# Two-stage kernel on one core: product two of the second channel product added in PSUM to a ScalarE copy of product one, one addition over two banks, gates directly behind their additions

## The chip, the cores and the metric

The kernel runs on one core of a Trainium2 chip. The metric is device time in microseconds of one execution. Each core has TensorE (PE, matmuls; "PEld" are its weight loads), VectorE (DVE), ScalarE (ACT), GpSimd (POOL) and SyncE (SP, which here only issues DMAs). Matmul results land in PSUM: eight banks of 128 partitions by 512 float32. SBUF is the other on-chip memory. Every engine works through its own queue in order, and engines wait for each other on semaphores.

## The reference

For each of 8 batches (S = 3008 rows, D = 256), with no softmax:

```python
scores = np.matmul(z, z.transpose(0, 2, 1)) / S        # d_qk = 64
x = u * np.matmul(np.maximum(scores, 0.0) ** 2, v)     # gated attention
h = np.maximum(x.transpose(0, 2, 1) @ w_tok1, 0.0) @ w_tok2    # token mixer, 256 wide
u = x + h.transpose(0, 2, 1)
out = u + np.maximum(u @ w_ch1, 0.0) @ w_ch2           # channel mixer, 1536 wide
```

Inputs and output are float32; the kernel multiplies in bfloat16 and accumulates in float32.

## The kernel before

**Blocks.** Queries are cut into six blocks `q` of 512 columns (the last has 448), so `b, q` names a block of a batch. Attention of a block: TensorE makes transposed scores `sc` (L470), ScalarE takes the relu into `at` (L508 or L496), VectorE squares it in place (L516 or L547), TensorE multiplies it with `v` into `acc` (L697). The matmuls of `sc` and `acc` use half of the array's rows and run in pairs, one on each half. Thus `acc` ends as two banks, which have to be added: ScalarE copies one bank to SBUF (`cp`, L825), VectorE adds the other to it (L831) and multiplies with u, the gate (L851, and L856 for the last 64 columns), into `xT`. That is `finish` and `gate`. The copies `cp` live in three buffers (`res`), which they share with `u_sb`, the turned-back u of the mixer.

**Mixer.** Per batch: the first token product `a_ps` (L1058) with a chain of small steps on ScalarE and VectorE into `a_f`; the second, `h_ps` (L1128), whose result VectorE adds to `xT` (L1137); the first channel product `hp` (L1192), in six steps of four matmuls a block, each with a relu into `h2pre` (L1231, ScalarE); sums and differences of the quarters of `h2pre` in `hsum` (`make_sums`, L1383, L1388, L1401, VectorE); and the second channel product.

**Second channel product.** It is done by a scheme that needs seven block products in place of eight, numbered 1 to 7 (`product`, L1447). Products 1, 2 and 3 take `h2pre` as it is, the others its sums `hsum`. In full blocks a product is 12 matmuls of 128 columns; in block q = 5 it is 6. Results stand in four quarters `ro` (upper or lower rows `m`, left or right columns `h`). Product 1 goes to a bank of the tile `xb`; products 6, 7 and 4 go on accumulating in that bank. Products 2 and 5 with 3 use the two banks of the tile `zb`. Behind each product, `collect` has VectorE add its bank to a quarter of `ro` (L1480), the first time together with `u_sb`. So 6 waits for the addition of 1, 7 for that of 6, 4 for that of 7 and 3 for that of 5. All this is done for 47 blocks; the very last (batch 7, q = 5) is multiplied out plainly (`op`, L1544), as are the last rows of other blocks with q = 5.

**The order of the work.** The program is written out by a planner in Python. It keeps a clock for each engine (`free`), lists of operations that wait for an engine (`push`: when ready, how long, `first` for rank, `room` for buffers) and lists of TensorE pieces (`heads` for the token part, `tails` for the channel part) with what each needs. It issues whatever can start first by its own durations. The real engines then follow that order with semaphores. Within `tails` the order is fixed by hand: a tuple per kind of block, in which a number is a product, 0 is the next step of the first channel product of block q + 1 (`add_next`, "a zero" below), and a to d are four stages of a grouped first step (`grouped_ch1`, tile `gp`, L1312) that needs ScalarE copies (L1320, L1323), relus (L1327, L1331) and one custom addition of VectorE (L1338). PSUM tiles of two banks come from a ring of four slots.

The plain order holds for 19 blocks (b = 0: q = 0 to 4; other batches: q = 3 and 4), the grouped one for 21 (b > 0, q = 0 to 2), and `ORDER_LAST` for seven with q = 5, where pieces of the next batch's `a_ps` may run between products. One zero of a block is left over and runs in front of the next block's order.

## Time and profile before

| | |
|---|---|
| three runs | 1110.31, 1108.81, 1110.19 us; median 1110.19 |
| the profiled execution | 1109.13 us, span of its instructions 1107.3 us |
| TensorE clock granted | 1.000 |
| busy: TensorE, VectorE, ScalarE | 1102.2, 811.5, 684.7 us |
| matmuls | 11199 |
| `ro` additions (L1480) | 329: 56.3 + 37.4 + 18.9 + 18.7 = 131.3 us |
| HBM read and written | 65.4 and 24.6 MB |

A row of the timeline reads: start in us from the span's start, length, engine, line, operation, output <- inputs, shape, xcount, and in brackets how long the engine was idle before and what ended that. A group's row reads: line, engine, operation, names, shapes, xcount, then busy us and mean ns of one, then the idle time before the group's instructions and what ended most of it. The length of a matmul row reaches past its last matmul's streaming time, so the distance between starts says more than the length. A row of the view by windows has the window, its length, and for PE, PEld, DVE, ACT and POOL the busy us and count, then clock and DMA.

### The profile page before, as it was taken

The numbers are of one execution on the slowest core, as the hardware profiler recorded it, in microseconds if no ns is written. First come the engines' busy times: TensorE is split into PE (matmuls) and PEld (weight loads), VectorE is DVE, ScalarE is ACT, GpSimd is POOL, SyncE is SP. The second block draws the span as 40 slices with busy tenths as digits, with TensorE's granted clock in tenths as the row PEclk, the third lists the DMA queues.
The fourth block names the chain that finished last, engine by engine and source line by source line (L and its number), as shares of the span: only waits on it lengthen the run. The fifth ranks groups of instructions, "written<-read, shape, count | busy, mean of one in ns | idle before, by whom it ended". The sixth has DMA issues, their size and how long they took to land.

```text
span 1107.3 us, 27459 instructions
## 1 busy us (share of the span) xinstructions
PE 1102.2 (100%) x11199; PEld 695.2 (63%) x11199; DVE 811.5 (73%) x1791; ACT 684.7 (62%) x906; POOL 168.2 (15%) x386
## 2 busy tenths in 40 slices
...
PEclk9999999999999999999999999999999999999999
...
GB/s 179 167 199 184 149 96 152 127 179 146 190 127 149 190 133 177 127 156 191 140 189 120 133 218 141 170 122 150 198 160 169 116 145 185 125 160 104 64 59 96
DMA packets 465726, 165.55 MB, mean 150 GB/s; under 512 B 433024, under 2 KB 448960, under 8 KB 465600
## 3 DMA queue, kind: packets, MB, share of 16 engines
...
q10 hardware_dynamic: 512, 0.38, 0.1%
...
## 4 chain that ended last, share of the span: by engine, by line
PE 99%; DVE 0%; ACT 0%; issue 0%
PE acc L697 42%; PE hp L1192 19%; PE xb L1447 11%; PE zb L1447 8%; PE sc L470 6%; PE h_ps L1128 4%; PE a_ps L1058 3%; PE gp L1312 3%; PE op L1544 2%; PE first_acc L614 1%; PE wp L210 0%; DVE at L516 0%; ACT at L508 0%; DVE zr L183 0%; PE first_acc L189 0%; DVE zT L1850 0%
## 5 line engine op out<-in xcount | busy, mean ns | idle before, releaser
L697 PEld LDWEIGHTS <-v_sb 64*128 64x128 bf16 x4418 | 245.7, 94 | 212.5 <-issue 1.3
L1231 ACT ACTIVATE h2pre<-hp 128x1024 bf16<-128x1024 f32 (+1 forms) x245 | 239.9, 1005 | 182.7 <-PE hp L1192 180.5
L697 PE MATMUL acc<-at,v_sb 64*128 64x512 bf16 (+1 forms) x2738 | 341.6, 374 | 0.0
L508 ACT ACTIVATE at<-sc 128x1024 bf16<-128x1024 f32 (+1 forms) x290 | 286.8, 1027 | 72.0 <-PE sc L470 66.4
L516 DVE TENSOR_TENSOR at<-at 128x1024 bf16<-128x1024 bf16 (+1 forms) x290 | 198.1, 687 | 112.1 <-ACT at L508 107.9
L1192 PE MATMUL hp<-xT,w_ch_sb 128*128 128x512 bf16 (+1 forms) x984 | 238.3, 374 | 0.0
L697 PE MATMUL acc<-fl,v_sb 64*128 64x512 bf16 (+1 forms) x1680 | 193.0, 367 | 0.0
L1192 PEld LDWEIGHTS <-w_ch_sb 128*128 128x128 bf16 x984 | 90.8, 98 | 79.0 <-issue 2.6
L1447 PEld LDWEIGHTS <-hsum 128*128 128x128 bf16 x2088 | 127.9, 98 | 19.6 <-issue 0.5
L470 PE MATMUL sc<-zT 64*128 64x512 bf16 (+1 forms) x732 | 132.4, 359 | 0.1
L1383 DVE TENSOR_TENSOR hsum<-h2pre 128x1024 bf16<-128x1024 bf16 (+1 forms) x141 | 90.0, 647 | 22.7 <-ACT h2pre L1231 12.6
L825 ACT COPY cp<-acc 128x512 f32<-128x512 f32 (+1 forms) x94 | 54.9, 584 | 79.9 <-PE acc L697 69.0
L831 DVE TENSOR_TENSOR cp<-acc,cp 128x512 f32<-128x512 f32 (+1 forms) x94 | 63.4, 675 | 54.8 <-ACT cp L825 54.0
L1447 PEld LDWEIGHTS <-h2pre 128*128 128x128 bf16 x1566 | 93.8, 98 | 10.0
L496 ACT ACTIVATE at<-sc 128x512 bf16<-128x512 f32 (+3 forms) x152 | 56.2, 450 | 29.2 <-PE sc L470 28.8
L1447 PE MATMUL xb<-shared_sb,hsum 128*128 128x128 bf16 x1044 | 73.6, 219 | 0.0
L1480 DVE TENSOR_TENSOR ro<-xb,u_sb 128x256 f32<-128x256 f32 (+1 forms) x141 | 56.3, 400 | 17.9 <-PE xb L1447 17.7
L470 PEld LDWEIGHTS <-zT 64*128 64x128 bf16 x732 | 42.4, 94 | 41.6 <-issue 3.8
L129 POOL CAST mark<-at 128x1 f32<-128x1 bf16 x24 | 9.3, 386 | 388.1 <-DVE at L516 388.1
L851 DVE TENSOR_TENSOR xT<-cp,uT 128x512 bf16<-128x512 f32 (+1 forms) x94 | 62.4, 663 | 0.8
L547 DVE TENSOR_TENSOR at<-at 128x512 bf16<-128x512 bf16 (+3 forms) x152 | 41.0, 320 | 23.8 <-ACT at L496 23.8
L1401 DVE TENSOR_TENSOR hsum<-h2pre,hsum 128x512 bf16<-128x512 bf16 (+1 forms) x141 | 55.1, 400 | 4.1 <-ACT h2pre L1331 2.5
...
## 6 DMA issues: line engine op xcount, KB each, us to landing
...
```

What stands on the lines that cost most here:

```text
L470: nc.tensor.matmul(sc[:, r, c0:c1], zT[h, k:k + P], zT[h, m + c0:m + c1], start=True, stop=True)
L496: nc.scalar.activation(a3[:, i, c0:c1], sc[:, r, c0:c1], ACT.Relu, scale=inv_S)
L508: nc.scalar.activation(view, sv, ACT.Relu, scale=inv_S)
L516: nc.vector.tensor_mul(view, view, view)
L697: nc.tensor.matmul(o, vs[blk.b, g][rows, i, dh * P:(dh + 1) * P], rhs, start=(dh, h) not in blk.begun, stop=stop, skip_group_check=True)
L831: nc.vector.tensor_add(cp[:, :W], acc[:, 0, :W], cp[:, :W])
L851: nc.vector.tensor_mul(xT[:, dh, :full * P].rearrange("p (t s) -> p t s", s=P), acc[:, :full * P].rearrange("p (t s) -> p t s", s=P), uT[: ...
L1192: nc.tensor.matmul(hps[r % len(hps)][:, r, :W], w_ch1_sb[:, dc, cc * P:(cc + 1) * P], xT[:, dc, :W], start=(dc == 0), stop=(dc == DT - 1))
L1231: nc.scalar.activation(h2[:, :, :W], hp[:, :, :W], ACT.Relu)
L1383: nc.vector.tensor_sub(sums["s"][:, 0:2, :, :n * P], h[:, :, 1], h[:, 0])
L1447: nc.tensor.matmul(to[:, i * P:(i + 1) * P], lhs, weights[:, c2, :], start=(first_use and c2 == 0 and i == 0), stop=(c2 == CHT // 2 - 1), ...
L1480: nc.vector.tensor_add(res(m, h), source, us(m, h) if opening else res(m, h))
```

## The change

Product 2 now goes to the second bank of `xb`. Behind product 1, ScalarE copies the first bank to the second (`fork`), and product 2 accumulates on that copy: the second bank then holds product 1 + product 2, while 6, 7 and 4 go on accumulating in the first. `zb` is opened at product 5 and uses one bank. The additions of 1 and 2 are gone; behind product 4 one addition takes both banks of `xb` and u into both upper quarters. Products 2 and 6 need the copy; product 2 also has to let reads of `xb` finish that are already issued (`Read`), and reads still waiting on VectorE are set behind it. The orders are new, and the planner's figure for the relu is 0.95 in place of 0.92. In the attention part the gate is ranked 0.12 us earlier, and a copy `cp` is issued only while copies and `u_sb` tiles together hold under three buffers.

In words, the plain order was (0, 0, 1, 2, 0, 6, 5, 0, 7, 3, 0, 4) and is (0, 1, 0, 5, 2, 6, 0, 0, 7, 0, 3, 4).

```diff
@@ -33,6 +33,17 @@
     @property
     def t(self):
         return None if self.done.t is None else self.done.t - self.us
+
+
+class Read:
+
+
+    def __init__(self, done):
+        self.done = done
+
+    @property
+    def t(self):
+        return self.done.t or 0.0
 
 
 class Op:
@@ -820,6 +831,7 @@
         on_act = blk.b > 0 or load("act") + 0.46 < load("dve") + 0.67
 
         def copy(t):
+            copies[0] += 1
             cp = sb.tile([P, QW], F32, tag="res", name="cp", bufs=3)
             if on_act:
                 nc.scalar.copy(cp[:, :W], acc[:, 1, :W])
@@ -829,16 +841,18 @@
 
         def add(cp, t):
             nc.vector.tensor_add(cp[:, :W], acc[:, 0, :W], cp[:, :W])
-            push("dve", t, 0.58, 0.7, lambda t: gate(blk, dh, cp, t), first=1,
+            push("dve", t - 0.12, 0.58, 0.7, lambda t: gate(blk, dh, cp, t), first=1,
                  room=(lambda: (blk.b, blk.q) in uTs and has_room(("xT",))) if dh == 0
                  else lambda: (blk.b, blk.q) in xTs)
 
         engine, busy = ("act", 0.46) if on_act else ("dve", 0.66)
-        push(engine, end + 0.21, busy, busy + 0.15, copy, first=1)
-
-    gated = [0]
+        push(engine, end + 0.21, busy, busy + 0.15, copy, first=1,
+             room=lambda: copies[0] + live["us"] < 3)
+
+    gated, copies = [0], [0]
 
     def gate(blk, dh, acc, t):
+        copies[0] -= not blk.whole
         b, q, W = blk.b, blk.q, blk.W
         uT = uTs[b, q]
         if dh == 0:
@@ -1021,9 +1035,11 @@
 
     hid_done = Done()
     BORROW = 3
-    GROUPED = ("a", 0, 1, 2, "b", 6, 5, 0, "c", 7, 3, 0, 4, "d")
+    RELU = 0.95
+    GROUPED = ('a', 0, 1, 0, 'b', 2, 6, 5, 'c', 7, 3, 0, 'd', 4)
+    PLAIN = (0, 1, 0, 5, 2, 6, 0, 0, 7, 0, 3, 4)
     VERY_LAST = (B - 1, NQ - 1, CHT // 2 - 1)
-    ORDER_LAST = ((1, 2, 6, 5, 7, 0, 3, 4), (1, 2, 6, 5, 0, 7, 3, 0, 4))
+    ORDER_LAST = ((1, 2, 6, 5, 7, 0, 3, 4), (1, 6, 0, 5, 2, 0, 3, 7, 4))
 
     def add_mixer(b):
         st = {}
@@ -1238,7 +1254,7 @@
                         late_sums.append(lambda t: make_sums(q, c2 // 2, t))
                     else:
                         make_sums(q, c2 // 2, t)
-            engine, busy = ("act", 0.92) if on_act else ("dve", 1.15)
+            engine, busy = ("act", RELU) if on_act else ("dve", 1.15)
             ring.append((push(engine, end + 0.21, busy, busy + 0.16, evacuate,
                               done=h2_done[q, c2]), slots[0]))
             if c2 == CHT // 2 - 1:
@@ -1414,9 +1430,9 @@
 
         def bank_of(q, k):
 
-            if k in (2, 5, 3):
-                return st["zb", q][:, int(k != 2)]
-            return st["xb", q][:, 0]
+            if k in (5, 3):
+                return st["zb", q][:, 0]
+            return st["xb", q][:, int(k != 2)]
 
         def product(q, k, end):
 
@@ -1425,7 +1441,7 @@
             if k == 1:
                 st["x_slot", q], _ = take_slot()
                 st["xb", q] = bank_pair(st["x_slot", q], "xb")
-            if k == 2:
+            if k == 5:
                 st["z_slot", q], _ = take_slot()
                 st["zb", q] = bank_pair(st["z_slot", q], "zb")
             to = bank_of(q, k)
@@ -1435,7 +1451,7 @@
             weights = {1: w2[:, :, 0, 0, :], 2: w2[:, :, 1, 0, :], 4: w2[:, :, 1, 1, :],
                        3: w_mix_sb[:, 3], 5: w_mix_sb[:, 0], 6: w_mix_sb[:, 1],
                        7: w_mix_sb[:, 2]}[k]
-            first_use = k in (1, 2, 5)
+            first_use = k in (1, 5)
             for c2 in range(CHT // 2):
                 d, j = divmod(c2, 2)
                 for i in range(n):
@@ -1452,6 +1468,11 @@
                 done_with_h2(q)
                 for d in range(CHT // 4):
                     release(home_of(q), [1], end + 0.2)
+            if k in (2, 6, 7, 4):
+                behind = [taken[q, j] for j in (1, 6, 7)]
+                for op in waiting["dve"]:
+                    if op.done in behind:
+                        op.ready = max(op.ready, end + 0.21)
             collect(q, k, end)
 
         def collect(q, k, end):
@@ -1467,19 +1488,33 @@
             def us(m, h):
                 return st["u", q][:, h, m * n:m * n + n, :]
 
-            blocks_of = {1: (0, 0), 2: (0, 0), 5: (1, 1), 6: (1, 0), 3: (1, 0), 7: (1, 1),
-                         4: (0, 1)}
-            opening = k in (1, 5, 6, 4)
+            blocks_of = {5: (1, 1), 6: (1, 0), 3: (1, 0), 7: (1, 1)}
+            begins = k in (6, 5, 4) and ("asked", q) not in st
+            if begins:
+                st["asked", q] = True
+
+            def fork(t):
+                nc.scalar.copy(bank_of(q, 2)[:, :n * P], bank_of(q, 1)[:, :n * P])
+
+            def first_column():
+                m, h = blocks_of.get(k, (0, 0))
+                return st["res", q][:, m * n, h * P:h * P + 1]
 
             def add(t):
-                if k == 1:
+                if begins:
                     home, n_home = take_home(q)
                     st["res", q] = sb.tile([P, QW // P, D], F32, tag=home, name="ro",
                                            bufs=n_home)
-                m, h = blocks_of[k]
-                nc.vector.tensor_add(
-                    res(m, h), source, us(m, h) if opening else res(m, h))
-                recent[0] = st["res", q][:, 0, :1]
+                if k == 4:
+                    nc.vector.tensor_add(
+                        st["res", q][:, :n, :].rearrange("p i (h d) -> p h i d", d=P),
+                        st["xb", q][:, :, :n * P].rearrange("p h (i d) -> p h i d", d=P),
+                        st["u", q][:, :, :n, :])
+                else:
+                    m, h = blocks_of[k]
+                    nc.vector.tensor_add(
+                        res(m, h), source, us(m, h) if k in (5, 6) else res(m, h))
+                recent[0] = first_column()
                 over[q] -= 1
                 if not over[q]:
                     nc.sync.dma_start(
@@ -1491,18 +1526,23 @@
             ready = end + 0.21
             done = taken[q, k]
             if k == 1:
+                push("act", ready, busy, busy + 0.15, fork, first=2, done=done)
+            elif k == 2:
+                pass
+            elif begins:
                 with_u(q, ready, lambda at: push(
                     "dve", at, busy, busy + 0.15, add, first=1, room=(home_of(q),),
                     frees=frees_of(q), done=done))
             else:
-                done = push("dve", ready, busy, busy + 0.15, add, first=1, done=taken[q, k],
-                            room=lambda: ("res", q) in st)
+                us_ = busy if k != 4 else 0.62 if n == 2 else 0.34
+                push("dve", ready, us_, us_ + 0.15, add, first=1, done=done,
+                     room=lambda: ("res", q) in st)
             if k == 3:
                 ring.append((done, st["z_slot", q]))
             if k == 4:
                 ring.append((done, st["x_slot", q]))
 
-        over = [7] * NQ
+        over = [5] * NQ
         us_uses = [[1] for _ in range(NQ)]
         s_done = {(q, d, k): Done() for q in range(NQ) for d in range(CHT // 4) for k in range(4)}
         taken = {(q, k): Done() for q in range(NQ) for k in range(1, 8)}
@@ -1641,8 +1681,10 @@
         def add_product(q, k):
             needs = {
                 1: [Sooner(h2_done[q, c], 0.111 * c) for c in range(CHT // 2)] + w_done[2:],
-                2: [], 5: [mix_done, taken[q, 2]], 6: [taken[q, 1]], 3: [taken[q, 5]], 7: [taken[q, 6]],
+                2: [taken[q, 1]], 5: [mix_done], 6: [taken[q, 1]], 3: [taken[q, 5]], 7: [taken[q, 6]],
                 4: [taken[q, 7]]}[k]
+            if k == 2:
+                needs = needs + [Read(taken[q, j]) for j in (6, 7)]
             kind = {5: 0, 7: 1, 6: 2, 4: 3}.get(k)
             if kind is not None:
                 needs = needs + [Sooner(s_done[q, d, kind], 0.222 * d) for d in range(CHT // 4)]
@@ -1650,7 +1692,7 @@
                 needs = needs + [tok1_over[b + 1]]
             cost = pairs_of(q) * (CHT // 2) * column_time(P)
             tails.append(Piece(cost, needs, lambda end: product(q, k, end), opens=k == 1,
-                               closes=k == 4, key=(b, 2 + q), slot=k in (1, 2),
+                               closes=k == 4, key=(b, 2 + q), slot=k in (1, 5),
                                joins=k == 1 and q == NQ - 1))
 
         added = [0] * (NQ + 1)
@@ -1670,7 +1712,7 @@
                 us_uses[q][0] += bool(rest)
                 h2_uses[q] += bool(rest)
                 for k in (ORDER_LAST[b % 2] if q == NQ - 1 else GROUPED if grouped(q + 1) else
-                          (0, 0, 1, 2, 0, 6, 5, 0, 7, 3, 0, 4)):
+                          PLAIN):
                     if isinstance(k, str):
                         add_grouped(q + 1, 0, "abcd".index(k), q)
                     elif k:
```

The lines below are in the order in which the engines' queues hold them. ScalarE in the first grouped cycle of batch 1, before; L1323 and L1320 belong to stage a, L1327 and the next L1320 to b, L1331 to d, L1231 are relus of `hp`:

```order
L1323 COPY s_3507<-gp 128x512
L1320 COPY gp<-gp 128x512
L1231 ACTIVATE h2pre<-hp 128x1024
L1327 ACTIVATE h2pre<-gp 128x512
L1320 COPY gp<-gp 128x512
L1231 ACTIVATE h2pre<-hp 128x1024 x2
L1331 ACTIVATE h2pre<-gp 128x512
L1231 ACTIVATE h2pre<-hp 128x1024
```

The same place after:

```order
L1339 COPY s_3506<-gp 128x512
L1336 COPY gp<-gp 128x512
L1497 COPY xb<-xb 128x256
L1247 ACTIVATE h2pre<-hp 128x1024
L1343 ACTIVATE h2pre<-gp 128x512
L1336 COPY gp<-gp 128x512
L1247 ACTIVATE h2pre<-hp 128x1024 x2
L1347 ACTIVATE h2pre<-gp 128x512
```

The copy of `xb` stands behind the copies of stage a and ahead of the relu of the zero in front of product 1.

VectorE in the second grouped cycle of batch 2, before (`ro<-xb,u_sb` are the additions of 1, then 6; `ro<-zb,ro` of 2, then 3; `ro<-zb,u_sb` of 5; `ro<-xb,ro` of 7; the `ISA` row is the custom addition behind stage c; `t_sums` prepare the next group):

```order
L1383 TENSOR_TENSOR hsum<-h2pre 128x1024
L1388 TENSOR_TENSOR hsum<-h2pre,hsum 128x512
L1480 TENSOR_TENSOR ro<-xb,u_sb 128x2x128
L1401 TENSOR_TENSOR hsum<-h2pre,hsum 128x512
L1480 TENSOR_TENSOR ro<-zb,ro 128x2x128
L1480 TENSOR_TENSOR ro<-xb,u_sb 128x2x128
L1480 TENSOR_TENSOR ro<-zb,u_sb 128x2x128
L1268 TENSOR_TENSOR t_sums<-xT 128x512
L1273 TENSOR_TENSOR t_sums<-xT,t_sums 128x256
L1338 ISA h2pre<-gp,s_5761 128x2x512
L1480 TENSOR_TENSOR ro<-xb,ro 128x2x128
L1480 TENSOR_TENSOR ro<-zb,ro 128x2x128
```

and after (L1515 are the additions of 6, 5, 7 and 3, L1509 the one over two banks):

```order
L1404 TENSOR_TENSOR hsum<-h2pre,hsum 128x512
L1417 TENSOR_TENSOR hsum<-h2pre,hsum 128x512
L1284 TENSOR_TENSOR t_sums<-xT 128x512
L1289 TENSOR_TENSOR t_sums<-xT,t_sums 128x256
L1294 TENSOR_TENSOR t_sums<-xT,t_sums 128x256
L1515 TENSOR_TENSOR ro<-xb,u_sb 128x2x128
L1515 TENSOR_TENSOR ro<-zb,u_sb 128x2x128
L1354 ISA h2pre<-gp,s_5704 128x2x512
L1515 TENSOR_TENSOR ro<-xb,ro 128x2x128
L1515 TENSOR_TENSOR ro<-zb,ro 128x2x128
L1399 TENSOR_TENSOR hsum<-h2pre 128x1024 x2
L1509 TENSOR_TENSOR ro<-xb,u_sb 128x2x2x128
```

The sums are no longer parted by additions of 1 and 2, and the `t_sums` stand ahead of the additions of 6 and 5.

VectorE in an attention stage, before:

```order
L831 TENSOR_TENSOR cp<-acc_6320,cp 128x512
L516 TENSOR_TENSOR at<-at 128x4x256
L851 TENSOR_TENSOR xT<-cp,uT 128x512
L831 TENSOR_TENSOR cp<-acc_6338,cp 128x512
L547 TENSOR_TENSOR at<-at 128x512
L547 TENSOR_TENSOR at<-at 128x384
L851 TENSOR_TENSOR xT<-cp,uT 128x512
```

and after:

```order
L843 TENSOR_TENSOR cp<-acc_6307,cp 128x512
L865 TENSOR_TENSOR xT<-cp,uT 128x512
L527 TENSOR_TENSOR at<-at 128x4x256
L843 TENSOR_TENSOR cp<-acc_6323,cp 128x512
L865 TENSOR_TENSOR xT<-cp,uT 128x512
L558 TENSOR_TENSOR at<-at 128x512
L558 TENSOR_TENSOR at<-at 128x384
```

Squares that stood between an addition and its gate now stand behind the gate.

## The prediction

> **What bounds the kernel now.** I read the page first, then TensorE's rows in order of time in the stages that the change touches, then VectorE's and ScalarE's rows in the same stages, and last the groups by form, for durations. The page:
>
> ```profile
> span 1107.3 us, 27459 instructions
> PE 1102.2 (100%) x11199; PEld 695.2 (63%) x11199; DVE 811.5 (73%) x1791; ACT 684.7 (62%) x906; POOL 168.2 (15%) x386
> PEclk9999999999999999999999999999999999999999
> PE 99%; DVE 0%; ACT 0%; issue 0%
> ```
>
> PE is busy throughout at a full granted clock, and the chain that ended last is PE. A busy PE could still hide short waits, because matmuls overlap. So I read starts, not busy times. This is one whole cycle of a mixer stage that runs in the order without groups, from one product 1 to the next:
>
> ```profile
> 880.12 0.83 PE L1447 MATMUL xb<-w_ch_sb,h2pre 128*128 128x128 bf16 x12
> 880.79 0.83 PE L1447 MATMUL zb<-w_ch_sb,h2pre 128*128 128x128 bf16 x12
> 881.46 1.03 PE L1192 MATMUL hp<-xT,w_ch_sb 128*128 128x512 bf16 x4
> 882.32 0.83 PE L1447 MATMUL xb<-shared_sb,hsum 128*128 128x128 bf16 x12
> 882.99 0.83 PE L1447 MATMUL zb<-shared_sb,hsum 128*128 128x128 bf16 x12
> 883.66 1.03 PE L1192 MATMUL hp<-xT,w_ch_sb 128*128 128x512 bf16 x4
> 884.53 0.83 PE L1447 MATMUL xb<-shared_sb,hsum 128*128 128x128 bf16 x12
> 885.20 0.83 PE L1447 MATMUL zb<-shared_sb,h2pre 128*128 128x128 bf16 x12
> 885.87 1.03 PE L1192 MATMUL hp<-xT,w_ch_sb 128*128 128x512 bf16 x4
> 886.73 0.83 PE L1447 MATMUL xb<-w_ch_sb,hsum 128*128 128x128 bf16 x12
> 887.40 2.54 PE L1192 MATMUL hp<-xT,w_ch_sb 128*128 128x512 bf16 x12
> 889.78 0.83 PE L1447 MATMUL xb<-w_ch_sb,h2pre 128*128 128x128 bf16 x12
> ```
>
> Each product takes 0.67 us from its start to the next start (56 ns a matmul), and each four hp matmuls 0.86 us (215 ns each). No row starts later than the one before allows: the cycle is streaming and nothing else. The changed kernel has the same 11199 matmuls, so time can be won only where PE waits. Read in this way, the mixer stages have 17 spots at which a matmul starts more than 20 ns late (switches between half and full rows of the array left out), 2.06 us together. The first, one of three of their kind and the last are these, with the VectorE row that ends the last:
>
> ```profile
> 127.28 2.76 PE L1128 MATMUL h_ps<-w_tok_sb,a_f 128*128 128x512 bf16 x12
> 129.97 1.02 PE L1192 MATMUL hp<-xT,w_ch_sb 128*128 128x512 bf16 x4
> ...
> 378.01 0.38 PE L1312 MATMUL gp<-t_sums,shared_sb 128*128 128x256 bf16 x2
> 378.32 0.83 PE L1447 MATMUL xb<-shared_sb,hsum 128*128 128x128 bf16 x12
> ...
> 1092.02 0.92 PE L1192 MATMUL hp<-xT,w_ch_sb 128*128 128x448 bf16 x4
> 1092.97 0.83 PE L1447 MATMUL xb<-shared_sb,hsum 128*128 128x128 bf16 x12
> ...
> 1092.50 0.42 DVE L1480 TENSOR_TENSOR ro<-xb,u_sb 128x256 f32<-128x256 f32 x1
> ```
>
> The last: four matmuls of 448 columns take 0.76 us (the twelve at 887.40 are four of 512 and eight of 448: 2.38 - 0.86 = 8 x 0.19), but product 6 starts 0.95 us after them, 0.05 us behind the end of the addition of product 1 (1092.92). That is a wait of 0.20 us. At 378.32 the same wait is 0.09 us. So what can be won is at most 2.06 us, 0.19% of 1109.13 us. Under 0.2%, some 2.2 us, I call the same: it is about what a measurement of this kernel can tell from no change.
>
> **The change, part by part.** Prices, by form, and how busy the others are in two cycles (a grouped one, then the one above):
>
> ```profile
> L1231 ACT ACTIVATE h2pre<-hp 128x1024 bf16<-128x1024 f32 x198 | 198.5, 1026 | 146.7 <-PE hp L1192 145.6 <-issue 1.1
> L831 DVE TENSOR_TENSOR cp<-acc,cp 128x512 f32<-128x512 f32 x78 | 53.5, 686 | 47.5 <-ACT cp L825 46.9
> L1480 DVE TENSOR_TENSOR ro<-xb,u_sb 128x256 f32<-128x256 f32 x120 | 50.3, 419 | 12.1 <-PE xb L1447 11.9
> L1320 ACT COPY gp<-gp 128x512 f32<-128x512 f32 x42 | 23.9, 570 | 1.3
> L1078 ACT COPY a_f<-a_ps 128x128 f32<-128x128 f32 x8 | 2.1, 265 | 33.7 <-PE a_ps L1058 33.7
> ...
> 384.05:394.58 10.53, 10.53 (x120) 8.01 (x118) 9.37 (x23) 7.57 (x11) 3.50 (x8) 1.00 1.13 204
> 880.12:889.78 9.66, 9.66 (x110) 7.03 (x109) 9.63 (x32) 5.88 (x7) 4.33 (x8) 1.00 0.96 161
> ```
>
> *Additions.* Of a cycle's seven (7 x 0.419 = 2.93 us) four stay, and one over two banks comes (0.686 by the 512-element row): 2.36. VectorE gains 0.57 us in a cycle, 0.57 x 40 full cycles = 23 us, and some 3 us in the seven narrow ones. PE waits for VectorE at few spots, so this is worth nothing by itself; if the two-bank read cost as much as two additions, VectorE would gain nothing and the end would not move either.
>
> *The copy.* ScalarE gains 40 copies of 256 elements. They lie between 0.265 us (128 elements) and 0.570 (512), on the line between them 0.367; 47 copies are some 17 us on an engine that is busy 62%. What counts is when the copy ends. Let L be a cycle's last hp (ended at 0), as in the rows above. An engine starts about 0.20 us behind the matmuls it waits for, and PE 0.05 us behind the engine:
>
> ```profile
> 387.99 0.83 PE L1447 MATMUL xb<-shared_sb,hsum 128*128 128x128 bf16 x12
> 388.66 0.83 PE L1447 MATMUL zb<-shared_sb,hsum 128*128 128x128 bf16 x12
> ...
> 390.19 0.38 PE L1312 MATMUL gp<-xT,shared_sb 128*128 128x256 bf16 x2
> 390.63 0.83 PE L1447 MATMUL xb<-shared_sb,hsum 128*128 128x128 bf16 x12
> ...
> 388.86 0.42 DVE L1480 TENSOR_TENSOR ro<-xb,u_sb 128x256 f32<-128x256 f32 x1 [0.54 <-PE xb L1447]
> ...
> 390.93 1.23 DVE L1338 CUSTOM_DVE_ANT_1 h2pre<-gp,s 128x1024 bf16<-128x1024 f32 x1 [0.31 <-PE gp L1312]
> ```
>
> In the new plain order (hp, 1, hp, 5, 2, 6 behind L): L's relu 0.20 to 1.23, the next hp's relu 1.23 to 2.26. Product 1 ends at 0.86 + 0.67 = 1.53, so the copy runs 2.26 to 2.63. Product 2 comes at 1.53 + 0.86 + 0.67 = 3.06: 0.38 us to spare. Product 2's cover is one hp and product 5. Were the copy as dear as the 512-element one, 0.18 would be left. Product 5 now comes second and needs the first sums, which no longer wait behind additions. Cost 0.
>
> *Product 1 comes one hp earlier.* Its last pair of matrices starts 0.86 + 0.56 = 1.42 behind L and L's relu is out at 1.28; where the hp between is 448 wide the margin is 0.04. At two places of batch 0, though, L is the third hp of an unbroken four: relus end at 0.20 + 3 x 1.03 = 3.29, and product 1 wants them at 3 x 0.86 + 0.56 = 3.14. With the 0.05 that is 0.20 us late, twice: **+0.40 us**. Before, a fifth hp stood there.
>
> *The grouped order.* Product 6's addition has to be out before product 7, and what lies between shrinks from 1.97 us (388.66 to 390.63) to product 5 and one stage, 0.67 + 0.44 = 1.11. The addition needs 0.20 + 0.42 + 0.05 = 0.67. With VectorE just begun on something of 0.69 it would be 0.25 late; in the order of VectorE's work above, the sums and t_sums stand ahead of it and are done, so 0. Product 7's addition waits behind the 1.23 us custom addition: out at 0.20 + 1.11 + 1.23 + 0.42 + 0.05 = 3.01 behind product 6, product 4 comes at 1.11 + 0.67 + 0.67 + 0.86 + 0.22 = 3.53. What goes is the wait for product 1's addition (378.32 and its like, three, 0.26 us; and 1092.97, 0.20): product 6 now follows product 2, which waits for ScalarE. **-0.46 us**.
>
> *The end of odd batches.* The token stage's first output needs ScalarE's a_f, and one op product moves ahead of the last token products:
>
> ```profile
> 361.27 1.47 PE L1544 MATMUL op<-w_ch_sb,h2pre 128*128 128x256 bf16 x12
> 362.58 0.50 PE L1447 MATMUL xb<-shared_sb,hsum 128*128 128x128 bf16 x6
> ...
> 364.56 0.81 PE L1128 MATMUL h_ps<-w_tok_sb,a_f 128*128 128x512 bf16 x3
> ...
> 363.07 0.42 ACT L1110 ACTIVATE a_f<-a_f 128x256 bf16<-128x256 f32 x1 [1.33 <-DVE a_f L1089]
> ```
>
> The token products end at 361.27, and a_f is ready at 363.54, 2.27 later; 3.29 us of PE work covers it. After, the cover is products 2, 3, 7 (0.33 each) and one op (1.31): 2.31. It holds by 0.04, at three places. Cost 0, at worst 0.2 each if an addition gets in front.
>
> *Copies held back, gates behind their additions.* In the attention stages this moves a square by one gate, 0.66 us. TensorE's rows there show no late start before that is worth naming, and squared tiles are made some way ahead of their use; a new wait of over 0.16 us (0.83 - 0.67) would show as idle time. The bounds are 0 and, if each of 94 gates cost TensorE 0.05 us, 4.7; I take 0, by those rows.
>
> **Sum**: 1109.13 - 0.46 + 0.40 = 1109.1 for the profiled execution (span 1107.3 and 1.8 around it). It lies 1.06 under the median of the runs, 1110.19, so on that scale 1110.1. With all 2.06 us of waits gone it would be 1108.1; with the thin margins (eight times 0.05 in front of product 1, three times 0.2 at the odd ends) 1111.1.
>
> [...] In the cycle at 880.12 VectorE is busy 9.63 us of 9.66 and weight loads 7.03. By row, PE's starts are gapless, so a free VectorE gives nothing there. If VectorE were the bound in spite of that, 26 us would come off: 1084. [...]
>
> **Rivals.** *The copy is late (slower).* ScalarE runs in order; if each copy stood behind one more relu of 1.03 us, product 2 would be 1.03 - 0.38 = 0.65 late in the 19 plain cycles: 12 us, 1122. It decides from 2.2 / 47 = 0.05 us a cycle on. For it: ScalarE has relus back to back there. Against: the order puts the copy ahead of the next relu, and 0.38 is to spare. *Product 6's addition is late (slower).* 21 grouped cycles at 0.25: 5 us, 1115; the cover was nearly halved; against it VectorE is 0.57 us lighter. Late squares in the attention stages give the same, 1115. *VectorE is the bound after all*: 1084. *More waits go than I can see* (in the start-up, which no step moves, or behind the page's rows): 1107.5.
>
> **How the numbers follow.** My forecast 0.76, the late copy 0.08, the late addition or squares 0.10, VectorE as the bound 0.02, more waits gone 0.04 (half of it beyond 0.2%). Faster: 0.02 + 0.02 = 0.04. Slower: 0.08 + 0.10 = 0.18. The same: 0.78. The range from 1107.9 to 1113.0 takes in both ends of the forecast and the milder half of the late additions.
>
> **What would show it.** Right: some 40 ScalarE copies of 256 elements near 0.37 us, VectorE busy near 786, ScalarE near 701; a plain cycle still 9.66 us from product 1 to product 1; product 2 starting 0.67 us behind product 5; late starts of 0.2 us at the two places in batch 0; none in front of product 6. Wrong: product 2 or 7 regularly starting late, or gaps in TensorE's rows in the attention stages.

## The result, and the profile after

The changed kernel takes 1110.93 us (median of 22 runs, 1110.44 to 1111.85), the kernel before, measured beside it, 1109.14 us (22 runs, 1108.81 to 1110.66). The ratio is 1.0016, with a 95% interval of 1.0010 to 1.0022: the change makes the kernel 1.8 us slower. The forecast was 1110.1 us on the scale of the first three runs, that is 0.06 us faster than before. The size stayed below the 0.2% that were called the same, but the sign is the other one, and the interval excludes no change.

The page of the changed kernel: span, busy times, granted clock, and the chain that ended last by engine.

```profile
span 1109.9 us, 27421 instructions
PE 1102.7 (99%) x11199; PEld 697.4 (63%) x11199; DVE 801.4 (72%) x1697; ACT 695.4 (63%) x953; POOL 171.3 (15%) x386
PEclk9999999999999999999999999999999999999999
PE 96%; DMA 2%; DVE 1%; issue 0%; ACT 0%; SPq 0%; DVEq 0%; ACTq 0%
```

TensorE is still the bound at a full clock (1.000 granted), but the chain now leaves it in places: 3% of it lie on DMAs and VectorE, where there was 1% for all others before. The new operations, in the view of groups by form:

```profile
L1497 ACT COPY xb<-xb 128x256 f32<-128x256 f32 x40 | 15.2, 380 | 0.1
L1509 DVE TENSOR_TENSOR ro<-xb,u_sb 128x512 f32<-128x512 f32 x40 | 27.4, 684 | 0.5 <-PE xb L1463 0.2
```

One plain cycle of the changed kernel in TensorE's rows in order of time, with ScalarE's copy of that cycle behind them:

```profile
881.22 0.83 PE L1463 MATMUL xb<-w_ch_sb,h2pre 128*128 128x128 bf16 x12
881.88 1.03 PE L1208 MATMUL hp<-xT,w_ch_sb 128*128 128x512 bf16 x4
882.75 0.83 PE L1463 MATMUL zb<-shared_sb,hsum 128*128 128x128 bf16 x12
883.42 0.83 PE L1463 MATMUL xb<-w_ch_sb,h2pre 128*128 128x128 bf16 x12
...
890.98 0.83 PE L1463 MATMUL xb<-w_ch_sb,h2pre 128*128 128x128 bf16 x12
...
882.38 0.39 ACT L1497 COPY xb<-xb 128x256 f32<-128x256 f32 x1
```

The cycle is as gapless as before: product 2 starts 0.67 us behind product 5, 0.65 us after the copy's end (882.77). It is 9.76 us long instead of 9.66 only because four of its hp matmuls that were 448 columns wide are now 512: 4 x (0.2157 - 0.1892) = 0.11.

So the 1.8 us are not in the cycles. To find them I cut TensorE's rows at the first matmul of each attention stage and compared the stretches between these starts (us, from the profiled executions):

| stretch | before | after | difference |
|---|---|---|---|
| start-up, to the steady scores | 23.91 | 24.18 | +0.27 |
| first attention stages and the start of batch 0's mixer | 140.85 | 141.27 | **+0.42** |
| batch 0 | 102.51 | 102.61 | +0.10 |
| batches 1, 3, 5 | 136.22, 136.26, 136.24 | 136.67, 136.70, 136.71 | **+0.45, +0.44, +0.47** |
| batches 2, 4 | 134.82, 135.03 | 134.83, 135.29 | +0.01, +0.26 |
| batches 6, 7 to the last matmul | 157.88 | 158.24 | +0.36 |

The three odd batches alone make 1.36 us. This is the end of the odd batch 1 in the changed kernel: TensorE's rows, then VectorE's.

```profile
363.38 1.47 PE L1584 MATMUL op<-w_ch_sb,hs 128*128 128x256 bf16 x12
364.69 0.50 PE L1463 MATMUL zb<-shared_sb,h2pre 128*128 128x128 bf16 x6
365.02 0.50 PE L1463 MATMUL xb<-shared_sb,hsum 128*128 128x128 bf16 x6
365.36 1.03 PE L1144 MATMUL h_ps<-w_tok_sb,a_f 128*128 128x512 bf16 x4
366.64 1.04 PE L1144 MATMUL h_ps<-w_tok_sb,a_f 128*128 128x512 bf16 x4 [0.26 <-DVE res L1623]
...
365.11 0.29 DVE L1124 TENSOR_SCALAR a_f<-a_f 128x256 bf16<-128x256 f32 x1
365.32 0.41 DVE L1623 TENSOR_TENSOR res<-op,u_sb 128x256 f32<-128x256 f32 x1
...
366.16 0.43 DVE L1623 TENSOR_TENSOR res<-op,u_sb 64x256 f32<-64x256 f32 x1
366.62 0.29 DVE L1515 TENSOR_TENSOR ro<-zb,ro 128x128 f32<-128x128 f32 x1
366.82 0.28 DVE L1515 TENSOR_TENSOR ro<-xb,ro 128x128 f32<-128x128 f32 x1
367.02 3.47 DVE L1153 TENSOR_TENSOR xT<-xT,h_ps 128x1024 bf16<-128x1024 bf16 x3
370.41 0.41 DVE L1509 TENSOR_TENSOR ro<-xb,u_sb 128x256 f32<-128x256 f32 x1
```

The first h_ps starts in time. The second starts 1.28 us behind it, where four matmuls take 0.86: 0.42 us late, until the four `res` additions are done. The same place in the kernel before:

```profile
365.43 0.50 PE L1447 MATMUL xb<-w_ch_sb,hsum 128*128 128x128 bf16 x6
365.76 1.46 PE L1128 MATMUL h_ps<-w_tok_sb,a_f 128*128 128x512 bf16 x6
...
363.75 0.28 DVE L1480 TENSOR_TENSOR ro<-zb,ro 128x128 f32<-128x128 f32 x1
364.76 0.42 DVE L1583 TENSOR_TENSOR res<-op,u_sb 128x256 f32<-128x256 f32 x1 [0.73 <-PE op L1544]
```

There the addition of product 3 (`ro<-zb,ro`) stood a microsecond ahead of the `res` additions, and the second h_ps followed without a pause. The stretches under the table's other bold number, and the small ones, come up with the experiments.

### The profile page after: what moved, and what is told of

It reads as the page before. It is cut to its first block, busy times and chain, and to the rows that moved or that the text cites. A ratio compares the mean times of both kernels' runs of the same rounds, so it can differ in the third digit from the quotient of the medians.

```text
span 1109.9 us, 27421 instructions
## 1 busy us (share of the span) xinstructions
PE 1102.7 (99%) x11199; PEld 697.4 (63%) x11199; DVE 801.4 (72%) x1697; ACT 695.4 (63%) x953; POOL 171.3 (15%) x386
## 4 chain that ended last, share of the span: by engine, by line
PE 96%; DMA 2%; DVE 1%; issue 0%; ACT 0%; SPq 0%; DVEq 0%; ACTq 0%
PE acc L708 42%; PE hp L1208 18%; PE xb L1463 13%; PE sc L481 6%; PE zb L1463 5%; PE h_ps L1144 4%; PE a_ps L1074 3%; PE gp L1328 3%; PE op L1584 1%; PE first_acc L625 1%; DMA at<-at 1%; DMA zT<-zr 1%; DMA out_dram<-ro 0%; DVE res L1623 0%; DVE a_f L1090 0%; DMA zf<-in_z_dram 0%
## 5 line engine op out<-in xcount | busy, mean ns | idle before, releaser
L1463 PEld LDWEIGHTS <-h2pre 128*128 128x128 bf16 x1566 | 97.2, 98 | 14.5
L1463 PE MATMUL xb<-w_ch_sb,h2pre 128*128 128x128 bf16 x1044 | 74.7, 219 | 0.0
```

The source lines that it names most:

```text
L1463: nc.tensor.matmul(to[:, i * P:(i + 1) * P], lhs, weights[:, c2, :], start=(first_use and c2 == 0 and i == 0), stop=(c2 == CHT // 2 - 1), ...
```

## The experiments

Waits below are read from the starts of single matmuls: what a start lies later than 0.216 us (512 columns) or 0.056 us (128 columns) behind the one before. Ratios are to the kernel before, measured on the same chip.

**The order at the end of odd batches put back.**

```diff
-    ORDER_LAST = ((1, 2, 6, 5, 7, 0, 3, 4), (1, 6, 0, 5, 2, 0, 3, 7, 4))
+    ORDER_LAST = ((1, 2, 6, 5, 7, 0, 3, 4), (1, 2, 6, 5, 0, 7, 3, 0, 4))
```

> The changed kernel with one tuple back: in odd batches the products of the block q = 5 stand again in the order (1, 2, 6, 5, 0, 7, 3, 0, 4). The copy, the two-bank addition, the new plain and grouped orders and the attention part stay. Theory one (at the odd ends product 3 and the last op piece end side by side, so two PSUM slots come free late and the second token output waits 0.42 us, and an hp behind it 0.10 us, three times): TensorE's wait inside h_ps goes at all three places, some 1.5 us of the 1.8 us go, ratio to the kernel before 1.0003 (1109.4 us). Theory two (the attention part is the cause): the odd order matters little, ratio 1.0012 to 1.0016. Theory three (copy and two-bank addition in the mixer cycles): the same ratio as theory two.

Measured: 1109.13 us, ratio 0.9996 [0.9987, 1.0005]. The odd batches take 136.13, 136.17 and 136.17 us, 0.07 to 0.09 less than before the change: the waits at the odd ends are gone, and so are the waits of product 6 behind product 1's addition. Most of the loss is in this tuple; the first stretch (141.28) and batch 0 (102.61) are as in the changed kernel.

**That order alone, on the kernel before.**

```diff
-    ORDER_LAST = ((1, 2, 6, 5, 7, 0, 3, 4), (1, 2, 6, 5, 0, 7, 3, 0, 4))
+    ORDER_LAST = ((1, 2, 6, 5, 7, 0, 3, 4), (1, 2, 6, 0, 5, 0, 3, 7, 4))
```

> The kernel before, without any copy, with the odd tuple alone changed to (1, 2, 6, 0, 5, 0, 3, 7, 4), so that product 3, product 7 and the last op piece stand as in the changed kernel. Theory one: the same wait of some 0.4 us inside h_ps at three places (batches 1, 3, 5), plus 0.1 us each behind it: 1.2 to 1.6 us slower than before, ratio 1.0011 to 1.0014. Theories two and three: no slower than before by more than 0.3 us, ratio 1.0000 to 1.0003.

Measured: 1111.71 us, ratio 1.0020 [1.0012, 1.0029]; odd batches 136.91 to 136.95. So neither copy nor two-bank addition is needed for a loss by this tuple. It is larger than theory one said (0.69 to 0.71 us an odd batch), and the waits are others: 0.19 us ahead of the first h_ps, then 0.11, 0.20 and 0.27 behind the second; the 0.42 us is not there. Batch 0 took 102.90 us, 0.39 more, although VectorE's, ScalarE's and SyncE's orders up to its end are those of the kernel before: VectorE waited 0.82 us there for a store of the output, and 0.43 before. Differences of this size can come from one execution to the next: the 22 runs of the kernel before alone spread over 1.85 us.

**The attention part taken out of the changed kernel.**

```diff
-            push("dve", t - 0.12, 0.58, 0.7, lambda t: gate(blk, dh, cp, t), first=1,
+            push("dve", t, 0.58, 0.7, lambda t: gate(blk, dh, cp, t), first=1,
-        push(engine, end + 0.21, busy, busy + 0.15, copy, first=1,
-             room=lambda: copies[0] + live["us"] < 3)
+        push(engine, end + 0.21, busy, busy + 0.15, copy, first=1)
```

> The changed kernel with the attention part undone: copies of an accumulator bank are issued without the limit on buffers, gates are not ranked 0.12 us earlier. Theory one: the waits at the odd ends stay, some 1.5 us; the two waits of 0.2 us in the first attention stage go: ratio 1.0012. Theory two: the loss goes, ratio 1.0000 to 1.0004. Theory three: ratio 1.0016, no change.

Measured: 1111.29 us, ratio 1.0017 [1.0009, 1.0026], nothing won in the sum. The stretches say why: the first one fell to 140.84 us (0.43 won), but batch 0 rose to 103.09 (0.48 lost).

**The attention part alone, on the kernel before.**

```diff
-            push("dve", t, 0.58, 0.7, lambda t: gate(blk, dh, cp, t), first=1,
+            push("dve", t - 0.12, 0.58, 0.7, lambda t: gate(blk, dh, cp, t), first=1,
-        push(engine, end + 0.21, busy, busy + 0.15, copy, first=1)
+        push(engine, end + 0.21, busy, busy + 0.15, copy, first=1,
+             room=lambda: copies[0] + live["us"] < 3)
```

The counter `copies` that goes with it is not shown.

> The kernel before with the attention part alone: the limit on copies and the gate ranked 0.12 us earlier. Theory one: 0.2 to 0.5 us slower, all of it in the first attention stage, where an addition that frees a PSUM slot now stands behind a gate: ratio 1.0002 to 1.0005. Theory two: ratio 1.0012 to 1.0016. Theory three: ratio 1.0000.

Measured: 1110.74 us, ratio 1.0016 [1.0005, 1.0028]. The first stretch is 141.28 (+0.43), as expected; batches 0, 2 and 4 gave 0.29, 0.36 and 0.35 more, at products 6 and 3 that waited for additions, which was not expected. They need not come from the attention part: the run with the odd order alone has a late product 6 in batch 0 too (0.25 us; here 0.35), behind VectorE's wait for a store of the output. I did not follow them further, since the changed kernel has other orders there.

**Product 3 ahead of the last op piece.** Here the slot that the second h_ps waits for should come free earlier.

```diff
-    ORDER_LAST = ((1, 2, 6, 5, 7, 0, 3, 4), (1, 6, 0, 5, 2, 0, 3, 7, 4))
+    ORDER_LAST = ((1, 2, 6, 5, 7, 0, 3, 4), (1, 6, 0, 5, 2, 3, 0, 7, 4))
```

> The changed kernel with one pair exchanged in the order that ends the odd batches: product 3 ahead of the last op piece, product 7 behind it. This puts product 3's addition back in front of the four res additions on VectorE and leaves the rest of the change as it is. Theory one (the second h_ps of batches 1, 3 and 5 waits for the PSUM slot that the last res addition frees, 0.42 us, and the next hp 0.10): the three waits of 0.42 are gone, each odd batch is 0.45 us shorter, the time about 1.4 us under the changed kernel's, a ratio to the kernel before of 1.000 to 1.0008. Theory four (it is not the slot but that op now opens behind product 2 instead of behind product 5, so that its last piece ends late): the waits stay at 0.3 us or more, the ratio 1.0012 to 1.002.

Measured: 1111.14 us, ratio 1.0012 [1.0003, 1.0021]: a miss. The wait of 0.42 us is gone, and the odd batches are as long as ever (136.71 and 136.72 in batches 3 and 5; 137.20 in batch 1, with one more wait of 0.55 us near 396 us, where VectorE waited 0.81 us for a store of the output). TensorE's and VectorE's rows at the end of batch 3:

```profile
636.97 1.89 PE L1144 MATMUL h_ps<-w_tok_sb,a_f 128*128 128x512 bf16 x8
638.78 0.49 PE L1463 MATMUL xb<-w_ch_sb,hsum 128*128 128x128 bf16 x6
...
639.97 1.03 PE L1208 MATMUL hp<-xT,w_ch_sb 128*128 128x512 bf16 x4
641.04 1.02 PE L1144 MATMUL h_ps<-w_tok_sb,a_f 128*128 128x512 bf16 x4
642.17 1.02 PE L1208 MATMUL hp<-xT,w_ch_sb 128*128 128x512 bf16 x4
...
638.64 3.47 DVE L1153 TENSOR_TENSOR xT<-xT,h_ps 128x1024 bf16<-128x1024 bf16 x3
642.03 0.42 DVE L1509 TENSOR_TENSOR ro<-xb,u_sb 128x256 f32<-128x256 f32 x1
```

Two h_ps now run in one piece, but product 4 is 0.08 us late, the fourth h_ps (641.04) 0.20 and the hp behind it (642.17) 0.27: 0.55 us in all, where the changed kernel lost 0.42 + 0.10. One slot alone does not explain that.

**Only the last op piece late.** My next theory was the length of VectorE's row behind `a_f`.

```diff
-    ORDER_LAST = ((1, 2, 6, 5, 7, 0, 3, 4), (1, 6, 0, 5, 2, 0, 3, 7, 4))
+    ORDER_LAST = ((1, 2, 6, 5, 7, 0, 3, 4), (1, 6, 0, 5, 2, 3, 7, 0, 4))
```

> The changed kernel with only the last op piece of the odd batches moved: behind products 3 and 7, so that it stands right before product 4 and the first h_ps, as it does before the change; the first op piece and product 2 stay where the change put them. The run with product 3 alone moved ahead lost the same 0.5 us per odd batch in other waits (0.08, 0.20 and 0.27 us), which theory one, the single slot, does not foresee. Theory five (VectorE's row behind a_f: the last op piece of 1.31 us is missing between the last a_ps and the first h_ps, so a_f, four res additions of 1.28 us in all and two product additions of 0.2 us each come just when the additions of h_ps should, and TensorE waits for that row): a_f is done 1 us before the first h_ps again, all these waits vanish, odd batches take 136.13 to 136.25 us instead of 136.70, and the time is 1.4 us under the changed kernel's, ratio 0.9995 to 1.0005 to the kernel before. Theory six (the first op piece, now behind products 1 and 6, or product 2 behind product 5, makes the end late): odd batches stay above 136.5, ratio 1.001 or more.

Measured: 1109.54 us, ratio 1.0000 [0.9991, 1.0008]; odd batches 136.33, 136.19, 136.19. The number came as theory five said, but its reason did not hold. The rows at the end of batch 3:

```profile
635.92 1.03 PE L1144 MATMUL h_ps<-w_tok_sb,a_f 128*128 128x512 bf16 x3
...
635.68 0.29 DVE L1124 TENSOR_SCALAR a_f<-a_f 128x256 bf16<-128x256 f32 x1
...
637.58 1.22 DVE L1153 TENSOR_TENSOR xT<-xT,h_ps 128x1024 bf16<-128x1024 bf16 x1
638.72 0.42 DVE L1509 TENSOR_TENSOR ro<-xb,u_sb 128x256 f32<-128x256 f32 x1
```

`a_f` is done no earlier against the first h_ps than in the changed kernel, and the first xT addition starts 1.66 us behind that h_ps (637.58 - 635.92), exactly as it did there (367.02 - 365.36). What differs is that products 3 and 7 are added ahead of the `res` additions, and that the two-bank addition of product 4 comes second, not fourth. Those are the additions that give back two of the four PSUM slots: `zb`'s and `xb`'s.

**Which slot: two instructions moved on VectorE.** The last theory was tested with TensorE's, ScalarE's and GpSimd's orders untouched (where the two-bank addition moves, a store of the output also moves ahead of one transpose in SyncE's queue). By its rank, product 3's addition goes ahead of the four `res` additions, or the two-bank addition goes from behind the third xT addition to behind the first, or both; the edit for both is

```diff
-                push("dve", ready, us_, us_ + 0.15, add, first=1, done=done,
-                     room=lambda: ("res", q) in st)
+                odd_end = q == NQ - 1 and b % 2
+                push("dve", ready - 0.6 * (odd_end and k in (3, 4)), us_, us_ + 0.15, add,
+                     first=3 if odd_end else 1, done=done, room=lambda: ("res", q) in st)
```

Both:

> The changed kernel with TensorE's, ScalarE's and GpSimd's orders left as they are; on VectorE two instructions move at each of the three odd ends: product 3's addition from behind the four res additions to ahead of them, and product 4's two-bank addition from behind the third xT addition to behind the first (on SyncE one transpose of u moves by one place). The run with the last op piece late removed the waits although its first xT addition began as late after the first h_ps as in the changed kernel (1.66 us), so that VectorE's row as a whole isn't the cause as theory five had it. Theory seven (two PSUM slots, given back late by VectorE's order: zb's, by product 3's addition, makes the second h_ps wait 0.42 us; xb's, by the two-bank addition, makes a later h_ps or hp wait 0.1 to 0.27 us): the waits of 0.42 and 0.10 us are gone, at most 0.1 us stays per odd end, odd batches take 136.15 to 136.30 us instead of 136.70, the time is 1.3 us under the changed kernel's, ratio 0.9995 to 1.0006 to the kernel before. Theory five in its own form (the length of VectorE's row): the second and third xT additions come 0.34 us later for the addition ahead of them, the waits stay at 0.5 us or more, ratio 1.001 or more.

Product 3's addition alone (`k == 3` in place of `k in (3, 4)`, and `first=3` for it only):

> The changed kernel with one instruction moved at each odd end: product 3's addition ahead of the four res additions on VectorE; every other engine's order and every queue is the changed kernel's. Theory seven (two PSUM slots): the second h_ps no longer waits 0.42 us, but xb's slot still comes back behind the third xT addition, so that the waits of the run with product 3 moved on TensorE appear in its place: 0.08 ahead of product 4, 0.20 ahead of the fourth h_ps, 0.27 ahead of the hp behind it; odd batches stay at 136.6 to 136.75 us, the time within 0.3 us of the changed kernel's, ratio 1.0008 to 1.002. If zb's slot alone were the cause: 136.15 to 136.3.

The two-bank addition alone (the same with `k == 4`):

> The counterpart: at each odd end only the two-bank addition moves, from behind the third xT addition to behind the first. Theory seven: the wait of the second h_ps for zb's slot, 0.42 us, stays; the 0.10 us ahead of the later hp goes; odd batches 136.55 to 136.65 us, ratio 1.0005 to 1.002. If xb's slot alone were the cause: 136.15 to 136.3.

What came, at each of the odd ends and in the odd batches without other waits:

| moved ahead | waits at the odd end, us | odd batch, us | ratio |
|---|---|---|---|
| nothing (the changed kernel) | 0.42 + 0.10 | 136.67 to 136.71 | 1.0016 [1.0010, 1.0022] |
| product 3's addition | 0.08 + 0.20 + 0.27 | 136.71 | 1.0016 [1.0008, 1.0025] |
| the two-bank addition | 0.42 | 136.57 to 136.61 | 1.0009 [1.0000, 1.0018] |
| both | 0.08 | 136.21 to 136.25 | 1.0033 [1.0021, 1.0046] |

With product 3's addition alone, batch 1 took 137.13 us; it has one more wait, 0.46 us near 396 us, again where VectorE waited for a store. The rows of batch 1 with both moved, TensorE's and then VectorE's (two `h_ps` of four matmuls in one piece, one of the eight records is missing):

```profile
364.56 1.89 PE L1144 MATMUL h_ps<-w_tok_sb,a_f 128*128 128x512 bf16 x7
...
364.52 0.28 DVE L1515 TENSOR_TENSOR ro<-zb,ro 128x128 f32<-128x128 f32 x1
...
367.35 0.42 DVE L1509 TENSOR_TENSOR ro<-xb,u_sb 128x256 f32<-128x256 f32 x1
```

The waits and the batches are as theory seven gave them: two slots come back late, and freeing one only uncovers the other. A word on what an output then waits for: the slot that VectorE gives back next. In the changed kernel that is op's slot for the second h_ps (366.64, behind the last `res` addition, which ends at 366.59; product 3's addition ends only at 366.91), and for the later hp the slot that the third xT addition frees (end 370.49, hp at 370.55).

The time of the kernel with both moves, 1113.37 us, missed by 3.8 us, though; it is 2.4 us over the changed kernel's 1110.93 (the next expectation says 3.5). In its profile the odd batches 1 and 5 took 136.55 and 136.25 us, batch 3 took 140.72, because of one stall of 2.8 us elsewhere. It was run once more beside the single moves:

> Both moves together once more, beside the two single ones on one chip. Where both moved, the waits at the three odd ends fell to 0.08 us, but the time was 3.5 us above the changed kernel's: in the profiled run a store of the output stood behind five transposes that took 18.4 us instead of 10 to 15, and VectorE waited 3.1 us for it. If that is this order's doing, it is here again: a stall of 1 us or more, ratio 1.0025 or more, and the run with the two-bank addition alone, which has the same order of stores and transposes, shows it too. If it came from that chip's transfers at that time: 1109.6 us, ratio 0.9995 to 1.0006.

Measured: 1112.71 us, ratio 1.0035 [1.0022, 1.0047], so it belongs to this order. In this second profile batch 1 took 136.21 us, batch 5 136.25 and batch 3 140.07. SyncE's rows of batch 3 in order of time, then VectorE's and TensorE's at the stall:

```profile
643.41 16.82 SPq L578 DMA_TRANSPOSE fl<-at  x5
...
662.54 0.53 SPq L1520 DMA_DIRECT2D out_dram<-ro  x1
...
667.07 0.69 DVE L1399 TENSOR_TENSOR hsum<-h2pre 128x1024 bf16<-128x1024 bf16 x1 [2.42 <-DMA out_dram<-ro]
...
668.41 1.68 PE L1208 MATMUL hp<-xT,w_ch_sb 128*128 128x512 bf16 x4 [1.99 <-DVE ro L1509]
```

The granted clock (the number behind POOL's) in the view by windows, behind the gap:

```profile
669.00:673.50 4.50, 4.50 (x34) 3.09 (x33) 2.15 (x6) 1.63 (x3) 0.65 (x3) 0.66 0.79 195
```

A store of the output stands behind five transposes in SyncE's queue, VectorE waits for its tile, and TensorE waits 2.16 us for VectorE. Of the 3.82 us that the batch is longer, the other 1.66 are a lowered clock behind the gap. The same store was issued at 659.91 with the two-bank addition alone, where there was no such stall, although the queue's order is the same: the part of the expectation on that kernel failed. Why the transposes take longer with both moves (16.8 and 18.4 us against 15.7) stays open. Shorter waits of VectorE for a store show in batch 1 of other kernels, as said above.

**The attention part in halves.** Both kernels have the order of before at the odd ends. The first takes back the gates' rank and keeps the limit on copies, the second the other way round.

```diff
-            push("dve", t - 0.12, 0.58, 0.7, lambda t: gate(blk, dh, cp, t), first=1,
+            push("dve", t, 0.58, 0.7, lambda t: gate(blk, dh, cp, t), first=1,
```

> The changed kernel with the order of before at the end of odd batches, and with the gates' rank put back (no 0.12 us earlier); the limit on copies held ahead of their gates stays. In the four runs so far the stretch from the first scores to the start of batch 0's attention products is 0.43 us longer wherever the attention part is in (three kernels) and not where it is out (three kernels). If the gate's earlier rank is the cause (an addition that frees a PSUM slot stands behind a gate at 100 us): the stretch is 0.43 us shorter here than with both. If the limit is the cause: no shorter. The wait of product 2 near 203 us was 0.14 us with both, 0.62 without: with the limit alone 0.14 if the limit keeps the cp copies off ScalarE there, 0.62 if the gates do. Time: 0.4 us under the kernel with both parts at best, a ratio of 0.9992 to 1.000 to the kernel before.

```diff
-        push(engine, end + 0.21, busy, busy + 0.15, copy, first=1,
-             room=lambda: copies[0] + live["us"] < 3)
+        push(engine, end + 0.21, busy, busy + 0.15, copy, first=1)
```

> The counterpart: the order of before at the end of odd batches, the gates' earlier rank kept, the limit on copies taken out. If the gate's rank costs the 0.43 us of the first stretch, they are here too; if the limit does, the stretch is as before. The wait of product 2 near 203 us: 0.62 us if the limit kept it short, 0.14 if the rank did. Time: a ratio of 0.9995 to 1.0008 to the kernel before.

Measured: 1109.49 us, ratio 0.9996 [0.9981, 1.0011], and 1109.30 us, ratio 0.9993 [0.9984, 1.0003]. First stretch: 140.84 with the limit alone, 141.28 with the rank alone. Wait of batch 0 near 203 us: 0.62 with the limit alone, 0.14 with the rank alone. The rank does both, the limit neither. The place in the first stretch, changed kernel, VectorE's rows and TensorE's:

```profile
99.61 0.69 DVE L865 TENSOR_TENSOR xT<-cp,uT 128x512 bf16<-128x512 f32 x1
100.22 0.68 DVE L843 TENSOR_TENSOR cp<-acc,cp 128x512 f32<-128x512 f32 x1
...
99.87 1.04 PE L708 MATMUL acc<-at,v_sb 64*128 64x512 bf16 x8
100.95 0.39 PE L481 MATMUL sc<-zT 64*128 64x512 bf16 x2
```

and with the limit alone:

```profile
99.57 0.69 DVE L843 TENSOR_TENSOR cp<-acc,cp 128x512 f32<-128x512 f32 x1
...
100.05 1.03 PE L708 MATMUL acc<-fl,v_sb 64*128 64x512 bf16 x8
100.91 0.38 PE L481 MATMUL sc<-zT 64*128 64x512 bf16 x2
```

With the early gates TensorE's scores start 1.08 us behind matmuls of 0.86 us, 0.05 behind the end (100.90) of an addition that frees a PSUM slot and stands behind a gate; another 0.20 us go at 86.5 us, for which the trace names no releaser. With the late gates the addition has begun at 99.57, and nothing waits.

The wait near 203 us is ScalarE's, in batch 0: product 1 needs the last of four relus, and these stand behind a copy `cp`. Rows of the kernel without the attention part, ScalarE then TensorE:

```profile
200.82 0.53 ACT L837 COPY cp<-acc 128x448 f32<-128x448 f32 x1 [0.60 <-DVE xT L869]
201.25 3.78 ACT L1246 ACTIVATE h2pre<-hp 128x1024 bf16<-128x1024 f32 x4
...
204.17 0.28 PE L1462 MATMUL xb<-w_ch_sb,h2pre 128*128 128x128 bf16 x2 [0.46 <-ACT h2pre L1246]
```

The copy waited for a gate on VectorE; with early gates it starts sooner.

**The best of each stretch together**: the order of before at the odd ends, late gates in batch 0 alone.

```diff
-            push("dve", t - 0.12, 0.58, 0.7, lambda t: gate(blk, dh, cp, t), first=1,
+            push("dve", t - 0.12 * (blk.b > 0), 0.58, 0.7, lambda t: gate(blk, dh, cp, t), first=1,
```

> The changed kernel with the order of before at the end of odd batches, and the gates' rank put back in batch 0 alone. It joins what the runs so far showed to cost least in each stretch: 140.84 us to the first attention products of batch 0 (against 141.28 with the early gates), 102.6 in batch 0 (with the early gates; 103.08 if the rank there is what decides), 136.1 in odd batches. Expected from the first scores on: 0.0 to 0.5 us over the kernel before, the time a ratio of 0.9995 to 1.0005 to it, 1.5 to 2.3 us under the changed kernel. If the waits moved only and did not vanish: 1110.5 or more.

Measured: 1109.06 us, ratio 0.9995 [0.9986, 1.0004]. The waits did vanish (140.97 and 102.61 us in the first two stretches, 0.12 us left near 101), the ratio fell from the changed kernel's 1.0016 to 0.9995, and against the kernel before nothing measurable is left. Copy and two-bank addition win TensorE nothing that these runs can tell.

**Product 2 right behind product 1**: the plain and the grouped order of before.

```diff
-    GROUPED = ('a', 0, 1, 0, 'b', 2, 6, 5, 'c', 7, 3, 0, 'd', 4)
-    PLAIN = (0, 1, 0, 5, 2, 6, 0, 0, 7, 0, 3, 4)
+    GROUPED = ("a", 0, 1, 2, "b", 6, 5, 0, "c", 7, 3, 0, 4, "d")
+    PLAIN = (0, 0, 1, 2, 0, 6, 5, 0, 7, 3, 0, 4)
```

> The changed kernel with the orders of before inside the plain and grouped cycles, so that product 2 stands right behind product 1 and has to wait for ScalarE's copy; nothing else is changed. It prices the wait that the new orders cover. Product 2 then starts after product 1's end, some 0.2 us to the copy's start and 0.39 to 0.43 us of copy, about 0.67 us late, in each of about 40 cycles that are not the last of a batch: 27 us more, a time of 1130 to 1142 us, if nothing takes the wait's place. If the copy is often ready or the scheduler puts other work between: under 1120.

Measured: 1144.94 us, ratio 1.0315 [1.0294, 1.0336], somewhat above the expected band. A cycle of batch 1, TensorE's rows and ScalarE's copy:

```profile
345.44 0.83 PE L1463 MATMUL xb<-w_ch_sb,h2pre 128*128 128x128 bf16 x12
347.12 0.83 PE L1463 MATMUL xb<-w_ch_sb,h2pre 128*128 128x128 bf16 x12 [0.84 <-ACT xb L1497]
...
346.65 0.42 ACT L1497 COPY xb<-xb 128x256 f32<-128x256 f32 x1
```

Product 1 ends its stream at 346.11, the copy starts behind a relu at 346.65, and product 2 is a microsecond late. Product 2 starts late at 40 places, by 0.66 to 1.27 us, 33.9 us in all and 0.85 each: the price that the new orders cover in full.

**The addition over two banks split in two.**

```diff
-                    nc.vector.tensor_add(
-                        st["res", q][:, :n, :].rearrange("p i (h d) -> p h i d", d=P),
-                        st["xb", q][:, :, :n * P].rearrange("p h (i d) -> p h i d", d=P),
-                        st["u", q][:, :, :n, :])
+                    for h in range(2):
+                        nc.vector.tensor_add(
+                            res(0, h),
+                            st["xb", q][:, h, :n * P].rearrange("p (i d) -> p i d", d=P),
+                            us(0, h))
```

> The changed kernel with the addition that reads two banks written as two additions of one bank each, as before the change; the copy and the orders stay. It gives VectorE back the time that the two-bank addition saves, about 0.1 us per cycle (0.69 against twice 0.40), some 5 us in all, and frees product 4's PSUM slot as much later. Theory: VectorE has that time to spare, the time stays within 0.5 us of the changed kernel's, ratio 1.001 to 1.002 to the kernel before; if VectorE's row is what TensorE waits for at the odd ends, the additions there add 0.07 to 0.1 us to each of the three. Rival (VectorE's time counts in full in the cycles): 4 to 5 us slower than the changed kernel, ratio 1.005 or more.

Measured: 1111.24 us, ratio 1.0019 [1.0010, 1.0027]; from the first scores to the last matmul 1082.19 us against 1082.32 in the changed kernel. VectorE is busy 804.1 us, 2.7 more, and TensorE doesn't notice, at the odd ends either (136.67 to 136.71; the 0.07 to 0.10 us foreseen there did not come).

## Why the prediction was right or wrong

**Gapless cycles, at most 2.06 us to win: right.** The plain cycle streams as before.

**"Additions", worth nothing: right in time, too large in size.** The rows' lengths fell by 25.8 us (131.3 to 105.5), but VectorE's busy time by 10.1, not 26 (801.4, where about 786 was named). Additions in a row start 0.33 us apart although a row is 0.42 long, and the next starts 0.60 us behind a two-bank addition, so each one saved gives back less than its length. That takes the 25.8 to some 18 (an estimate from these distances, as if all stood in a row); the other 8 are not explained. The split addition shows that TensorE does not feel VectorE's sum (2.7 us more of it, and 1082.19 us against 1082.32 from the first scores to the last matmul). The measurement also decides against VectorE as the bound: its busy time fell by 10.1 us, and the kernel's time rose by 1.8.

**"The copy", cost 0: right.** 0.380 us where 0.367 was worked out, ScalarE 695.4 where 701 was named, and product 2 never waits in the plain cycles. Without its cover a copy costs 0.85 us; the rival of the late copy was priced at 0.65.

**"Product 1 comes one hp earlier", +0.40: mis-sized.** Late starts came at one of the two places, 0.14 us. The term took each of three relus as 1.03 us, their rows' length; in a row of four they start 0.92 us apart (3.78 - 1.02 over three). What stayed late at 203 us is due to a copy `cp` ahead of them, which the term did not contain; without the earlier gates it is 0.62 us, so that the small 0.14 is luck of another part.

**"The grouped order", -0.46: right in its waits, too large by a third.** The three waits of product 6 and the one at 1092.97 are gone and products 6 and 7 wait nowhere in it; but a new wait of 0.29 us inside product 5 of the last cycle takes the place of 0.20 and 0.09 there (1067.87 and 1092.97 before), so that some 0.3 us stay won, the one at 217.25 (0.055) included. (One reading behind this step is off without harm: in the rows shown, the custom addition starts 0.30 us behind its matmuls, not 0.20; the margin of product 7's addition was 0.52.)

**"The end of odd batches", cost 0: this is the step that failed.** It counted the TensorE work that covers `a_f`, found a margin of 0.04 us, and that was right: the first h_ps is in time. It didn't count what the move does on VectorE. With the last op piece ahead of products 3 and 7, the `res` additions stand ahead of theirs, product 4 and its two-bank addition slide behind the second h_ps and the third xT addition, and two of four PSUM slots come back too late for the outputs behind the first, which wait for the next slot that VectorE frees. Cost 0.52 us, three times; with 0.09 won at each of them by the grouped order, the 0.45 of the table. The prediction's "at worst 0.2 each" named the right place and the wrong wait.

**"Copies held back, gates behind their additions", cost 0: wrong by 0.43 us in the first stretch, near 0 in the sum by luck.** The step looked at squares behind a gate. What waits at 101 us (0.22 of the 0.43) is an addition behind a gate, which frees the slot for the next scores; what waits at 86.5 us is open. The same earlier gates spare batch 0 some 0.48 us, which the step did not foresee either, so that the kernel without them is no faster (1.0017 against 1.0016). The 0.43 lies inside the bounds that were given (0 to 4.7).

In sum, by the stretches against the kernel before: 3 x 0.45, 0.43 in the first stretch and 0.10 in batch 0 are 1.9 us, and the medians differ by 1.8. The time lies in the range because the range is wide; the sum had a loss of 1.35 us at nothing. The profiled execution's further 0.26 us (VectorE waited 0.53 us for a store), 0.36 (attention matmuls behind transposes) and 0.27 in the start-up came in no regular way in the other kernels, so they are not put down to the change.
